# Two fold buffers, row-wise adds, whole K heads and planned idle in a two-layer decode kernel

## The chip, the core and the metric

The kernel runs on one core of a Trainium2 chip. Five engines work from instruction streams of their own and meet through semaphores: TensorE (PE in the profile; its weight loads are listed as PEld), VectorE (DVE), ScalarE (ACT), GpSimd (POOL) and SyncE (SP), which here only issues DMAs. The metric is the device time of one execution in microseconds (us).

## The reference

One decode step for four batch rows: attention over a long cache, a gated feed-forward block, and both once more with the same weights and the same cache. With the shapes filled in:

```python
# x (4,1,512); k_cache, v_cache (4, 8, 8192, 128); wq (512, 4096); wo (4096, 512)
# w_gate, w_up (512, 1792); w_down (1792, 512); all bf16
def _A_ref(x, k_cache, v_cache, wq, wo):          # 32 query heads, 8 K/V heads, Dh = 128
    q = (x @ wq).reshape(B, 1, 32, 128).transpose(0, 2, 1, 3)
    k = repeat(k_cache, 4, axis=1); v = repeat(v_cache, 4, axis=1)
    p = softmax(einsum("bhqd,bhkd->bhqk", q, k) * 128 ** -0.5)
    o = einsum("bhqk,bhkd->bhqd", p, v)
    return o.transpose(0, 2, 1, 3).reshape(B, 1, 4096) @ wo
def _B_ref(x, w_gate, w_up, w_down):
    return (silu(x @ w_gate) * (x @ w_up)) @ w_down
x = x + _A_ref(layernorm(x), ...)
x = x + _B_ref(layernorm(x), ...)
x = x + _A_ref(layernorm(x), ...)
x = x + _B_ref(layernorm(x), ...)
```

## The kernel before

**Tiling.** K and V of one batch row and one K/V head are 2 MiB. They are cut into two units of 1 MiB (`cp` 0 and 1, 8 KB in each of 128 partitions). A unit is written (layer, row, head, cp). A ring of 11 slots of 1 MiB (`pool`) holds units; four more slots lie in `wq_sb` and become free when the last query projection has read wq. `load_unit` fetches one unit, `load_both` fetches a whole head, two units with 16 KB in each partition, into two neighbouring slots: slot pairs are (0,1), (2,3) and so on, so the eleventh slot has no partner. Weights have places of their own (wo in four pieces, gate, up and down in two pieces each). A block is one layer and one row; the blocks run in the order `KSEQ`: (0,0), (0,1), (1,0), (0,2), (1,1), (0,3), (1,2), (1,3). Of each row's V the first three heads (six units, `KEPT`) stay in their slots from layer 0 until layer 1 has used them; they are loaded once.

**A block.** For each K unit, DVE transposes its two halves in place in 32x32 pieces (`k_pair`, L621), then PE multiplies them with the padded query `qpad` (32 matmuls, L633; called QK below). The scores of the whole block gather in four PSUM banks. `softmax` then takes maxima on DVE (L651), exponentials on ACT (L655), joins the maxima over partitions with a matmul against `same` (`g2`, L673), rescales (L691), transposes p on PE and copies it back on ACT (L700, L706), and forms the inverse sums (L715 to L731). Each V head is two units of eight matmuls (`v_group`, L787; called PV below), whose result is spread over four partition strips; `fold` on DVE adds the four strips into the buffer `red` under a mask (one L810 and three L813), `flip` on PE turns `red` into columns (L819), `nm` scales them (L828) and `oproj` multiplies with wo (L750). The very last head has no fold and multiplies the other way round (L773), and its second unit comes in two halves, so that the end is short. All four folds, flips and heads share the one buffer `red`.

**A chain.** When all eight heads of a layer 0 row are projected, `chain` runs serially on PE, DVE and ACT: `add_x` adds the residual (L931), then come a layer norm (L457 to L485), gate and up (L844), the gating (L862 to L883), down (L893), `add_x` again, another layer norm, the query projection for layer 1 (L493) and the padding of the query (L506, L533). Only then can QK of that row's layer 1 block run. `add_x` writes all four rows of XT each time, of which a chain uses its own. After block (1,3) the same feed-forward runs once for all rows and ends the kernel.

**What sets the order.** Two things. The string `ORDER` gives the order in which SyncE issues loads: each K and V stands for the next unit of `kseq` or `vload` (nothing more is issued for the second unit of a head fetched whole), q for wq, e for the last half unit, every other letter for the next weight piece. `VGROUPS` gives the order of V heads and marks with w those fetched whole. And `Plan` runs an event model of the kernel while it is being built: every step has an engine, an assumed duration, the steps it depends on and a priority; the earliest startable step of each engine is placed next, a free PSUM bank or slot is handed out on the way, and `emit` writes all instructions in the order of planned starts. So each engine's program order is fixed by the plan; `_Sync` adds the semaphore waits at emission. A load waits on SyncE until its slot's last reader is done, and all later loads queue behind it. Chain steps and softmax steps have the highest priority, but a step that has begun is never interrupted. In this order of emission nothing keeps a second fold from being written ahead of the first one's flip.

Of the kernel before, what the change touches and what calls it, by code (L numbers as in the profile page):

```python
# [4 lines left out]
ACTF = mybir.ActivationFunctionType  # L5
# [97 lines left out]
class Step:  # L103
    __slots__ = ("eng", "us", "deps", "fn", "prio", "take", "free", "start", "end", "loads", "slot_of", "slots", "pairs", "more")

    def __init__(self, eng, us, fn, deps, prio, take=None, free=None, pairs=0):
        self.eng, self.us, self.fn, self.prio = eng, us, fn, prio
        self.pairs = pairs
        self.deps = [d for d in deps if d is not None]
        self.take, self.free = take, free  # L110
        self.start = self.end = None
        self.slot_of = None
        self.slots = ()
        self.more = ()


class Plan:
# [6 lines left out]
    FETCH = 6.0  # L124

    def __init__(self, nslots, banks):
# [4 lines left out]
        self.bank = {}  # L131

    def add(self, eng, us, fn, deps, prio, take=None, free=None, pairs=0):
        s = Step(eng, us, fn, deps, prio, take, free, pairs)
        self.steps.append(s)
        return s
# [8 lines left out]
    def run(self):  # L145
# [12 lines left out]
        held = {}  # L158
        slots = {i: 0.0 for i in range(self.nslots)}
# [49 lines left out]

        def pump(now):  # L210
# [22 lines left out]
        left = len(self.steps)  # L233
        pump(0.0)
        while left:
            best = None
            for e in engines:
                cand = None
                for t, s in todo[e]:
                    if s.take is not None:  # L240
# [3 lines left out]
                        t = max(t, b)  # L244
                    at = max(t, free_at[e])
                    k = (at > free_at[e] + 1e-9, at if at > free_at[e] + 1e-9 else 0.0, s.prio[0])
# [5 lines left out]
            if li < len(self.loads):  # L252
                if not self.loads[li].slots:
                    nxt = sp_at
                else:
                    found = pick(self.loads[li])
                    nxt = found[0][0] if found is not None else None
            if best is None and nxt is None:
# [4 lines left out]
            at, s = best  # L263
            s.start = at
# [6 lines left out]
            if s.take is not None:  # L271
# [3 lines left out]
                self.bank[s.take] = b  # L275
            if s.free is not None:
# [11 lines left out]
    def emit(self):  # L288
        for s in sorted(self.steps + self.loads, key=lambda s: (s.start, s.prio[0])):
# [3 lines left out]
ORDER = ("qKKKKKVKKKKKKVKKKKdKVKVKKVKKKKVKKKVKVVVVKgKKVKKuVdVoVuogooVVKKKKKKKKKKVKKKKKKVVVVKVKKKVKVKKVKKKK"  # L293
         "VVVKKVVVVVVKVVVKVKKVVKKVKKKKKKKKKKKKKVVVVKKVVKVVVKKKKVVVVVVVVVVKVKKVVVKKKKKKKVVKKVKKKKVKKKKVKKKK"
         "KVVVVVVVVVVVVVVVVVKKVKKKKKKKKKKKKKKVVVVVVVVVVVVVVVVe")
KEPT = [6, 6, 6, 6]
NSLOT = 11
VGROUPS = ("006w 007w 004w 001w 003w 005w 002w 000w 016w 015w 014 013w 112w 011w 012w 017w 010w 121w 105w 107 101 104w 103 106 "
           "120 110w 023 027 021w 026w 025w 100w 130 024w 022w 020w 116 113 115 114 117 035 033 036 034w 032w 031 037w "
           "030 125w 123w 111w 131w 132 127w 124w 133w 134w 122 102 135w 137w 136 126")  # L300


def bass_interleave_layers__gqa_block_cached__swiglu_ffn__decode_kernel(
# [33 lines left out]
    with ExitStack() as es:  # L337
# [11 lines left out]
        tiny = sb("tiny", [P, 28], FP32)  # L349
# [3 lines left out]
        var = tiny[:, 9:13]  # L353
        rstd = tiny[:, 13:17]
        eps_sb = tiny[:, 17:18]
        gm = tiny[:, 18:19]
        gl = tiny[:, 19:20]
        cmask = tiny[:, 20:24]
        gm4 = tiny[:, 24:28]
        identf = sb("identf", [P, P], FP32)  # L360
        same = sb("same", [P, P], FP32)
# [5 lines left out]
        red = sb("red", [P, P], FP32)  # L367
        x0T = sb("x0T", [P, NQ, B], FP32)
        XT = sb("XT", [P, NQ, B], FP32)
        dT = sb("dT", [P, NQ, B], FP32)  # L370
# [9 lines left out]
        gs2 = sb("gs2", [P, FO * B], FP32)  # L380

# [35 lines left out]
        def setup_late():  # L417
            op("dve", lambda e: e.tensor_reduce(same[:, 0:32], identf[:].rearrange("p (c h) -> p h c", c=4),
                                                AX.X, ALU.add), reads=["identf"], writes=["same"])
            s0 = same[:]  # L420
            op("dve", lambda e: e.tensor_copy(s0[:, 32:P].rearrange("p (c h) -> p c h", h=32),
                                              bass.AP(tensor=s0.tensor, offset=s0.offset,
                                                      ap=[[s0.ap[0][0], P], [0, 3], [1, 32]])),
               reads=["same"], writes=["same"])
# [43 lines left out]
        def layer_norm(dep, tag):  # L468
# [6 lines left out]
            def square():  # L475
                op("dve", lambda e: e.tensor_tensor(dT[:], XT[:], over_nq(mean), ALU.subtract),
                   reads=["x", "mean"], writes=["dT"])
# [654 lines left out]
```

## Time and profile before

| | before |
|---|---|
| median of 3 runs | 643.45 us (642.36 to 643.55) |
| the profiled execution | 642.89 us |
| its span | 641.1 us |
| mean granted TensorE clock | 0.688 |
| from HBM through the DMA queue of SyncE | 257.18 MB |
| loads of K: 1 MiB each | 128 |
| loads of V: 2 MiB and 1 MiB | 34 and 35 (and two halves) |

The span runs from the first to the last instruction. Busy shares are means over the whole span. A group's row gives line, engine, operation, output from input, count, then total busy time in us and mean ns of one, then the idle time of the engine in front of it and what ended it. A row of a timeline gives start and length in us, engine, line and count, and in square brackets the idle time before it with what ended it. A row of SyncE's waits gives total us, times and longest.

### The profile page before, as it was taken

What the parts mean: (1) busy time and instruction counts of PE and PEld (TensorE: products, weight loads), DVE (VectorE), ACT (ScalarE), POOL (GpSimd) and SP (SyncE); (2) the same over time, 40 slices, a digit from 0 to 9 for tenths busy, and PEclk for the clock granted to TensorE, in tenths of its full rate; (3) what the DMA queues carried; (4) which work ended last, traced back from release to release, by engine and by line L of the source; (5) the groups of instructions that cost most, each with busy time, mean ns of one, the idle gap of its engine ahead of it and who ended that gap; (6) DMA issues with size and microseconds to landing.
All of it is one profiled execution on the core that took longest, in us unless ns stands there. A gap on an engine that the chain in (4) does not pass through costs nothing.

```text
span 641.1 us, 17218 instructions
## 1 busy us (share of the span) xinstructions
PE 451.4 (70%) x7882; PEld 207.6 (32%) x7882; DVE 451.7 (70%) x817; ACT 48.3 (8%) x114; POOL 1.6 (0%) x7
## 2 busy tenths in 40 slices
PE   2656666474777767679777766797757677976787
PEld 2211322133422322245322432362312335522345
DVE  2787885672599769646998857379988844798553
ACT  1000300030000300000300300000200200000300
POOL 0000000000000000000000000000000000000000
PEclk9866588565586678665767687576586875588575
DMA  8999999999999999999999999999999999999991
GB/s 362 422 421 410 420 423 423 403 401 392 383 398 410 421 422 426 423 423 406 410 420 420 422 425 429 417 406 421 419 408 421 406 420 415 331 413 427 427 416 53
DMA packets 36368, 258.27 MB, mean 403 GB/s; under 512 B 3396, under 2 KB 9288, under 8 KB 10568
## 3 DMA queue, kind: packets, MB, share of 16 engines
q1 hardware_dynamic: 36272, 257.18, 97.7%
q8 instruction: 61, 1.00, 0.6%
q14 instruction: 11, 0.09, 0.0%
q10 hardware_dynamic: 24, 0.01, 0.0%
HBM read 257.17 MB, written 0.00 MB: 401 GB/s over the span
## 4 chain that ended last, share of the span: by engine, by line
DMA 54%; DVE 22%; PE 16%; SPq 5%; issue 3%; DVEq 0%
DMA pool<-in_A_k_cache_dram 37%; DVE pool L621 15%; DMA pool<-in_A_v_cache_dram 14%; PE ps L633 5%; PE ps L787 5%; SPq L92 5%; DVE red L813 4%; DMA wd_sb<-in_B_w_down_dram 3%; DVE red L810 1%; PE ps L844 1%; PE ps L819 1%; PE ps L493 1%; PE ps L893 1%; PE ps L457 1%; PE ps L750 1%
## 5 line engine op out<-in xcount | busy, mean ns | idle before, releaser
L621 DVE STREAM_TRANSPOSE pool<-pool 128x1024 uint32<-128x1024 uint32 x244 | 288.1, 1221 | 49.4 <-DMA pool<-in_A_k_cache_dram 44.3
L633 PE MATMUL ps<-pool,qpad 32*32 32x512 bf16 x3904 | 217.6, 519 | 69.5 <-DVE pool L621 62.9
L633 PEld LDWEIGHTS ps<-pool,qpad 32*32 32x32 bf16 x3904 | 64.0, 106 | 203.0 <-DVE pool L621 136.3
L787 PE MATMUL ps<-pool,pp 128*32 128x512 bf16 x960 | 97.4, 526 | 32.9 <-DMA pool<-in_A_v_cache_dram 29.0
L813 DVE SCALAR_TENSOR_TENSOR red<-ps,tiny,red 128x128 f32<-128x128 f32 x189 | 66.3, 351 | 6.7
L810 DVE TENSOR_SCALAR red<-ps,tiny 128x128 f32<-128x128 f32 x63 | 21.4, 340 | 64.1 <-PE ps L787 53.7
L819 PE MATMUL ps<-sel,red 128*128 128x4 f32 x126 | 30.9, 318 | 46.5 <-DVE red L813 45.4
L819 PEld LDWEIGHTS ps<-sel,red 128*128 128x128 f32 x126 | 25.7, 256 | 78.4 <-DVE red L813 70.6
L655 ACT ACTIVATE pp<-ps,negm 128x512 bf16<-128x512 f32 x32 | 21.6, 685 | 304.2 <-DVE negm L651 297.4
L787 PEld LDWEIGHTS ps<-pool,pp 128*32 128x32 bf16 x960 | 22.3, 111 | 67.7 <-DMA pool<-in_A_v_cache_dram 39.9
L651 DVE TENSOR_REDUCE negm<-ps 128x1 f32<-128x512 f32 x32 | 19.8, 682 | 10.8 <-PE ps L633 10.8
L750 PE MATMUL ps<-oT,wo_sb 128*128 128x4 bf16 x640 | 21.9, 166 | 4.8 <-DVE oT L828 3.2
L750 PEld LDWEIGHTS ps<-oT,wo_sb 128*128 128x128 bf16 x640 | 21.2, 104 | 11.5 <-DVE oT L828 4.7
L493 PE MATMUL ps<-xnT,wq_sb 128*128 128x4 bf16 x640 | 18.4, 166 | 8.8 <-DMA wq_sb<-in_A_wq_dram 8.0
L493 PEld LDWEIGHTS ps<-xnT,wq_sb 128*128 128x128 bf16 x640 | 18.2, 104 | 10.9 <-DMA wq_sb<-in_A_wq_dram 8.1
L483 ACT ACTIVATE tiny<-tiny 128x4 f32<-128x4 f32 x10 | 3.0, 300 | 233.5 <-DVE tiny L463 233.5
L828 DVE TENSOR_TENSOR oT<-ps,invL 128x4 bf16<-128x4 f32 x64 | 9.7, 151 | 14.2 <-PE ps L819 13.3
L706 ACT ACTIVATE pp<-ps 128x1024 bf16<-128x1024 bf16 x16 | 16.1, 1023 | 29.4 <-PE ps L700 29.4
L700 PE MATMUL ps<-ident,pp 128*128 128x128 bf16 x128 | 14.9, 296 | 0.5 <-DVE invL L731 0.3
L700 PEld LDWEIGHTS ps<-ident,pp 128*128 128x128 bf16 x128 | 11.9, 137 | 9.1 <-DVE selw L719 4.2
L621 DVE STREAM_TRANSPOSE wq_sb<-wq_sb 128x1024 uint32<-128x1024 uint32 x12 | 14.2, 1224 | 0.5
L633 PE MATMUL ps<-wq_sb,qpad 32*32 32x512 bf16 x192 | 11.1, 516 | 4.9 <-DVE wq_sb L621 4.8
(73 smaller groups left out, 171.6 us busy)
## 6 DMA issues: line engine op xcount, KB each, us to landing
pool<-in_A_k_cache_dram SPq DMA_DIRECT2D x122, 1024.0 KB, 10.2
pool<-in_A_v_cache_dram SPq DMA_DIRECT2D x31, 2048.0 KB, 13.2
pool<-in_A_v_cache_dram SPq DMA_DIRECT2D x35, 1024.0 KB, 9.5
wq_sb<-in_A_k_cache_dram SPq DMA_DIRECT2D x6, 1024.0 KB, 12.6
wq_sb<-in_A_v_cache_dram SPq DMA_DIRECT2D x3, 2048.0 KB, 17.5
wq_sb<-in_A_wq_dram SPq DMA_DIRECT2D x1, 4096.0 KB, 12.5
wo_sb<-in_A_wo_dram SPq DMA_DIRECT2D x4, 1024.0 KB, 19.4
wg_sb<-in_B_w_gate_dram SPq DMA_DIRECT2D x2, 896.0 KB, 15.7
```

Of the source, the lines that this page charges most:

```text
L92: ins = self.eng[engname].dma_start(out_ap, in_ap)
L493: op("pe", lambda e: e.matmul(ps[:, bk * BW + h * B:bk * BW + (h + 1) * B], lhsT=wq_sb[:, kt, h * Dh:(h + 1) * Dh], rhs=xnT[:, kt * B:(kt ...
L621: op("dve", lambda e: e.transpose(v, v), reads=[key], writes=[key])
L633: op("pe", lambda e: e.matmul(ps[32 * c:32 * (c + 1), a * BW:(a + 1) * BW], lhsT=qpad[rows, es_, g, :], rhs=ap[h][rows, :, es_ // 2, :, es ...
L651: op("dve", lambda e: e.tensor_reduce(negm[:, q, a:a + 1], bank(a), AX.X, ALU.max, negate=True), reads=[f"pb{a}"], writes=[f"negm{q}_{a}"])
L655: op("act", lambda e: e.activation(pblk(q)[:, :, a, :], bank(a).rearrange("p (t j) -> p t j", j=32), ACTF.Exp, bias=negm[:, q, a:a + 1], s ...
L700: op("pe", lambda e: e.matmul(stg[:, t * P:(t + 1) * P], lhsT=pp[:, q, blk * P:(blk + 1) * P], rhs=ident[:], is_transpose=True, start=True ...
L750: op("pe", lambda e: e.matmul(ps[:, OPJ * BW + nq * B:OPJ * BW + (nq + 1) * B], lhsT=wo_sb[:, h, nq * P:(nq + 1) * P], rhs=o_cols(l, h), s ...
L787: op("pe", lambda e: e.matmul(ps[32 * j:32 * (j + 1), bk * BW:(bk + 1) * BW], lhsT=pp[:, q, at:at + 32], rhs=ap[:, 4 * j * Dh:4 * (j + 1) ...
L810: op("dve", lambda e: e.tensor_scalar(red[:], blk, mask4[:, t:t + 1], None, op0=ALU.mult), reads=[f"pb{bk}", "mask4"], writes=["red"])
L813: op("dve", lambda e: e.scalar_tensor_tensor(red[:], blk, mask4[:, t:t + 1], red[:], op0=ALU.mult, op1=ALU.add), reads=[f"pb{bk}", "mask4" ...
L819: op("pe", lambda e: e.matmul(ps[:, bk * BW:bk * BW + REP], lhsT=red[:], rhs=sel8[:, REP * (g % 2):REP * (g % 2 + 1)], start=True, stop=True),
```

## The change

- `red` gets a second half. A fold takes one of the two (`hold`) when it is planned and the flip gives it back (`drop`); a fold can be planned only when a half is free, and its half is free again when the flip ends.
- `add_x` gets the rows it may write: a chain's own row, and all four at the end. So in layer 0 each chain now leaves the other rows of XT as they are.
- To make room, `same` shrinks from 128 to 32 columns and one copy in the setup goes; `g2` becomes four matmuls of 32 columns, one for each partition strip. `var` and `dT` share places with `rstd` and `gs`.
- The K units of a block come head by head (cp 0 and 1 of one head together), and 25 K heads, all of layer 0, are loaded whole.
- The plan can leave an engine idle ahead of a step of a chain or a softmax: `LOOK` gives each of the four chains and eight softmaxes an index into `AHEAD`; a step that is in no such group isn't started when it would still be running at the expected start of a group's step that is less than so many us away. Four softmaxes have a value over 0: (0,0) 1.6, (1,0) 0.3, (1,1) 0.6, (1,3) 0.3; the chains have 0.
- `ORDER` and `VGROUPS` are new. Loads and bytes are the same in sum: 245.25 MiB through the queue. The stream now begins with wo0 and a whole K head ahead of wq. The last load of (0,3) ends at 209.25 MiB in both; after it came the V heads (1,2,5) and (1,2,3) and then the 16 K units of (1,3), and now come the heads (1,2,7), (1,2,5) and (1,2,3) with two of the K units among them, and then the other 14. The last K unit ended at 229.25 MiB and now ends at 231.25.

```diff
+        self.side = {}
+        self.ahead = [self.AHEAD[int(c)] for c in LOOK]      # AHEAD = (0.0, 0.3, 0.6, 1.0, 1.6)
...
+        def expected(s, depth):
+            t = 0.0
+            for d in s.deps:
+                x = d.end
+                if x is None:
+                    if depth == 0 or d.group is None:
+                        return None
+                    x = expected(d, depth - 1)
+                    if x is None:
+                        return None
+                    x = max(x, free_at[d.eng]) + d.us
+                t = max(t, x + (self.HOP if d.eng != s.eng else 0.0))
+            return t
+
+        def due():
+            found = {e: [] for e in engines}
+            for k, g in enumerate(self.groups):
...
+                    x = expected(s, 3)
+                    if x is not None:
+                        found[s.eng].append((x, self.ahead[k]))
+            return found
...
+                    if s.hold is not None:
+                        if not sides:
+                            continue
+                        t = max(t, min(sides.values()))
                     at = max(t, free_at[e])
+                    if s.group is None and any(at + s.us > x + 0.05 and x - at < w for x, w in soon[e]):
+                        continue
...
+            if s.drop is not None:
+                sides[self.side[s.drop]] = s.end + self.HOP
...
-ORDER = ("qKKKKKVKKKKKKVKKKKdKVKVKKVKKKKVKKKVKVVVVKgKKVKKuVdVoVuogooVVKKKKKKKKKKVKKKKKKVVVVKVKKKVKVKKVKKKK"
-         "VVVKKVVVVVVKVVVKVKKVVKKVKKKKKKKKKKKKKVVVVKKVVKVVVKKKKVVVVVVVVVVKVKKVVVKKKKKKKVVKKVKKKKVKKKKVKKKK"
-         "KVVVVVVVVVVVVVVVVVKKVKKKKKKKKKKKKKKVVVVVVVVVVVVVVVVe")
+ORDER = ("oKqKKKKKKKKKKKKKKVKKVKVVKVKVKKKKVKKVKVKVVKVVKVdoVKVuggouKodVKKKKKKKKKKKVKKVKKKVVVVVVKKVKKVKVKKVV"
+         "VVVKVVKVKKVVVKKKKKKVVKKVKKKKKKKKKKKKKKVVVVVVKVVKKKVKKVVKKKKKKKVVVVVVVVKKVVKKVVVVKKKKVKVKKKKKKKKKK"
+         "VVVVVVVVVVVVVVVVVVKVVVKKKKKKKKKKKKKKKVVVVVVVVVVVVVVe")
...
+LOOK = "000040102001"
+KWHOLE = "000 001 002 003 004 005 006 007 010 011 012 013 014 015 016 017 020 022 023 031 032 033 034 035 036"
...
-        red = sb("red", [P, P], FP32)
+        red = sb("red", [P, 2, P], FP32)
...
             def g2():
                 bk = pbk(n + "a")
-                op("pe", lambda e: e.matmul(ps[:, bk * BW:bk * BW + 4], lhsT=same[:], rhs=gm4[:], start=True, stop=True),
-                   reads=["gm4", "same"], writes=[f"pb{bk}"])
-            s = PL.add("pe", 0.51, g2, [s], CHAIN, take=n + "a", pairs=2)
+                for c in range(4):
+                    op("pe", lambda e: e.matmul(ps[32 * c:32 * (c + 1), bk * BW:bk * BW + 4], lhsT=same[:], rhs=gm4[:],
+                                                start=True, stop=True, tile_position=(0, 32 * c)),
+                       reads=["gm4", "same"], writes=[f"pb{bk}"], sig=(c == 3))
+            s = PL.add("pe", 0.6, g2, [s], CHAIN, take=n + "a", pairs=8)
...
             def fold():
-                bk = pbk(tag)
+                bk, r = pbk(tag), PL.side[tag]
...
-                        op("dve", lambda e: e.tensor_scalar(red[:], blk, mask4[:, t:t + 1], None, op0=ALU.mult),
-                           reads=[f"pb{bk}", "mask4"], writes=["red"])
+                        op("dve", lambda e: e.tensor_scalar(red[:, r, :], blk, mask4[:, t:t + 1], None, op0=ALU.mult),
+                           reads=[f"pb{bk}", "mask4"], writes=[f"red{r}"])
...
-                op("dve", lambda e: e.tensor_tensor(XT[:].rearrange("p n b -> p (n b)"), base[:].rearrange("p n b -> p (n b)"),
-                                                    ps[:, bk * BW:bk * BW + NQ * B], ALU.add),
+                got = ps[:, bk * BW:bk * BW + NQ * B].rearrange("p (n b) -> p n b", b=B)
+                op("dve", lambda e: e.tensor_tensor(XT[:, :, rows], base[:, :, rows], got[:, :, rows], ALU.add),
                    reads=[key, f"pb{bk}"], writes=["x"])
...
-        kseq = [("k", l, b, g, cp) for l, b in KSEQ for cp in range(NCP) for g in range(G)]
+        kseq = [("k", l, b, g, cp) for l, b in KSEQ for g in range(G) for cp in range(NCP)]
...
+        twin |= {("k",) + tuple(int(c) for c in x) for x in KWHOLE.split()}
```

## Predicted, before the changed kernel was run

> **What bounds the kernel now.** I read the page first (busy shares, the forty slices, the DMA queue, the chain that ended last), then the table of stages in 16 us and 4 us windows, SyncE's own timeline and waits, and last the timeline of two places: the end of layer 0's last batch row and the tail.
>
> ```profile
> span 641.1 us, 17218 instructions
> ...
> PE 451.4 (70%) x7882; PEld 207.6 (32%) x7882; DVE 451.7 (70%) x817; ACT 48.3 (8%) x114; POOL 1.6 (0%) x7
> ...
> GB/s 362 422 421 410 420 423 423 403 401 392 383 398 410 421 422 426 423 423 406 410 420 420 422 425 429 417 406 421 419 408 421 406 420 415 331 413 427 427 416 53
> ...
> q1 hardware_dynamic: 36272, 257.18, 97.7%
> ...
> DMA 54%; DVE 22%; PE 16%; SPq 5%; issue 3%; DVEq 0%
> ...
> L621 DVE STREAM_TRANSPOSE pool<-pool 128x1024 uint32<-128x1024 uint32 x244 | 288.1, 1221 | 49.4 <-DMA pool<-in_A_k_cache_dram 44.3
> ...
> pool<-in_A_k_cache_dram SPq DMA_DIRECT2D x122, 1024.0 KB, 10.2
> pool<-in_A_v_cache_dram SPq DMA_DIRECT2D x31, 2048.0 KB, 13.2
> ```
>
> No compute engine is over 70% and the DMA queue is busy 97.7%: this is one long stream from HBM. Its undisturbed rate is about 421 GB/s, so a MiB takes 2.49 us. At that rate 257.18 MB take 611 us; the rest of the span, 30 us, is the tail after the last byte (about 14: the last row below carries 80 GB/s x 16 us = 3.0 us of stream, so it ends near 627), the first slice (362, worth 2.2) and dips. The change moves no byte out of the stream, so it can only win in the dips, in the rate, or in the tail.
>
> ```profile
> 160.00:176.00 16.00, 11.92 (x279) 7.89 (x287) 7.92 (x20) 0.51 (x2) 0.00 (x0) 0.50 0.97 385
> 176.00:192.00 16.00, 11.99 (x240) 3.88 (x240) 15.88 (x14) 0.00 (x0) 0.00 (x0) 0.82 1.00 398
> ...
> 320.00:336.00 16.00, 11.10 (x201) 3.36 (x208) 15.28 (x15) 0.00 (x0) 0.00 (x0) 0.70 1.01 421
> ...
> 512.00:528.00 16.00, 12.20 (x138) 5.80 (x135) 8.43 (x30) 1.68 (x2) 0.00 (x0) 0.71 1.01 427
> ...
> 576.00:592.00 16.00, 9.72 (x208) 3.07 (x208) 15.11 (x13) 0.00 (x0) 0.00 (x0) 0.91 1.02 427
> 592.00:608.00 16.00, 11.32 (x107) 5.25 (x95) 7.96 (x25) 5.13 (x11) 0.00 (x0) 0.50 1.01 428
> 608.00:624.00 16.00, 13.57 (x194) 6.72 (x187) 9.37 (x30) 0.00 (x0) 0.00 (x0) 0.73 1.00 417
> 624.00:640.00 16.00, 11.91 (x315) 9.69 (x312) 5.90 (x25) 0.76 (x3) 0.00 (x0) 0.59 0.20 80
> ```
>
> The columns are PE, weight loads, DVE, ACT, POOL, granted clock, DMA share, GB/s. The deepest dip, the slice of 331, is layer 0's last chain, in 4 us windows:
>
> ```profile
> 544.00:548.00 4.00, 4.00 (x109) 2.76 (x106) 1.31 (x6) 0.05 (x1) 0.00 (x0) 0.50 0.75 252
> 548.00:552.00 4.00, 4.00 (x33) 1.63 (x27) 2.66 (x9) 0.00 (x0) 0.00 (x0) 0.50 0.96 332
> 552.00:556.00 4.00, 3.62 (x101) 3.42 (x99) 3.89 (x10) 0.51 (x2) 0.00 (x0) 0.50 1.01 371
> 556.00:560.00 4.00, 3.46 (x110) 2.09 (x115) 4.00 (x8) 0.00 (x0) 0.00 (x0) 0.50 0.98 389
> 560.00:564.00 4.00, 4.00 (x97) 1.55 (x81) 4.00 (x5) 0.00 (x0) 0.00 (x0) 0.76 0.98 365
> ```
>
> **Term 1, the dip of chain 3.** Against 421 these five windows miss 169, 89, 50, 32 and 56 GB/s; times 4 us over 421 that is 3.8 us. SyncE shows why:
>
> ```profile
> 533.05 1.45 SPq L92 DMA_DIRECT2D pool<-in_A_k_cache_dram  x1
> ...
> 546.09 5.79 SPq L92 DMA_DIRECT2D pool<-in_A_k_cache_dram  x4
> ```
>
> ```profile
> SPq L62 <- PE ps L787: 13.0, 2, 12.5
> ```
>
> Six of the 11 slots hold kept V units of row 3; after two 2 MiB V loads and one K the queue stands 12.5 us for a PV to free one, and nothing else is issued. The old order then has only K of (1,3), whose QK needs the chain's query; the new order places three V heads of (1,2) there (6 MiB instead of 4) among the first two K units. The first wait stays: five slots are five slots. But what two freed slots are given next is V that PE can use at once, so 2 MiB, up to 5.0 us of streaming, fall into the windows from 548 on, which miss 2.2 us. I take -2.0; ends 0 (PE is busy all 4.00 us of the first two windows and the PVs come no sooner) and -3.8.
>
> **Term 2, 25 whole K heads.** 25 loads of 2 MiB take the place of 50: 52.4 MB, of which each byte gets a better rate or not. With whole V heads in the stream I read 427 and 428, with single K 421: 52.4 MB differ by 1.9 us. But 576 to 592, where the last single K land, has 427 too. Ends 0 and -1.9; I take the middle, -1.0. The 25 issues saved on SyncE are hidden, since its queue runs ahead of the stream. A pair's first half is usable later: the 2 MiB rows land 13.2 us after issue against 10.2, so each first half sits some 2.5 to 3 us more in its slot. That is cover, not time, as long as pairs come free early (rival B).
>
> The Trainium skill, DMA: Bandwidth & Descriptors, "Why a DMA increments its semaphore by 16 and not by 1", says that only the full count of 16 means all data has landed, and an intermediate value doesn't tell which bytes have; so nothing of a pair can start before its last byte. The 13.2 against 10.2 agrees. It speaks against this part; by it alone term 2 would give nothing, the last K would land 1.0 later, and the sum would end at 642.2.
>
> **Term 3, other dips.** Chain 0, 160 to 192, misses 36 and 23 GB/s, 2.2 us. The weights and the end of wd1 stand at 61.25 MiB of the stream in both orders, and a V pair and single K of (1,0) follow in both. 0; ends -2.2 and +2.2. At the start wq now lands after 7 MiB, not 4 (+7.5 us), so the first QK moves from 19.6 to about 27:
>
> ```profile
> 19.60 3.40 PE L633 MATMUL ps<-pool,qpad 32*32 32x512 bf16 x64 [0.90 <-DVE qpad L533]
> ```
>
> By then 4.5 MiB of K have landed and 4 to 5 are in flight, inside 11 slots; DVE transposes meanwhile. 0; end +2.5 (one K unit late).
>
> **Term 4, the chain's own instructions.** The setup copy (L421) goes; row-wise adds keep their count, on a smaller tile; 0, and at most a tenth of a us over the kernel. The maximum over partitions (L673) turns from one 128-wide fp32 matmul, two passes, into four 32-wide ones, eight passes, in each of 8 softmaxes.
>
> ```profile
> L673 PE MATMUL ps<-tiny,same 128*128 128x4 f32 x16 | 4.5, 354 | 5.1 <-DVE tiny L667 5.1
> ...
> L506 PE MATMUL ps<-qT,ident 128*32 128x16 bf16 x256 | 3.5, 179 | 2.0 <-DVE qT L545 1.5 <-DVE qT L557 0.5
> ```
>
> The nearest 32-wide row costs 3.5 / 256 = 14 ns each in a burst, so six more cost +0.1; the other end is six at the old pace, 4.5 / 16 = 0.28 each, +1.7. I take +0.2, and only the last softmax's is on the path; the other seven lie under the stream.
>
> **Term 5, two fold buffers and planned idle.** In 'red' a second fold already runs ahead of the first flip:
>
> ```profile
> 532.16 1.12 DVE L813 SCALAR_TENSOR_TENSOR red<-ps,tiny,red 128x128 f32<-128x128 f32 x3
> ...
> 533.78 1.12 DVE L813 SCALAR_TENSOR_TENSOR red<-ps,tiny,red 128x128 f32<-128x128 f32 x3
> ...
> 534.96 0.59 PE L819 MATMUL ps<-sel,red 128*128 128x4 f32 x2 [1.53 <-DVE red L813]
> ```
>
> ```profile
> DVE red L810 <- PE ps L819: 9.8, 11, 3.1
> ```
>
> So the plan loses no freedom by the new rule; a flip no longer waits for a foreign fold, and 9.8 us of DVE waiting for flips go. Under the stream both are worth 0. So is the planned idle, at most 1.6 us ahead of a step, which holds the non-chain work behind it (transposes on DVE, QK and PV on PE). Without that cover it costs its own length. Where these count is the tail.
>
> **The tail decides how much of the gain is paid out.**
>
> ```profile
> 586.93 4.85 DVE L621 STREAM_TRANSPOSE wq_sb<-wq_sb 128x1024 uint32<-128x1024 uint32 x4
> 591.84 1.90 PE L633 MATMUL ps<-wq_sb,qpad 32*32 32x512 bf16 x31 [0.52 <-DVE wq_sb L621]
> 593.81 2.48 DVE L651 TENSOR_REDUCE negm<-ps 128x1 f32<-128x512 f32 x4 [2.02 <-PE ps L633]
> ...
> 606.27 3.60 PE L787 MATMUL ps<-pool,pp 128*32 128x512 bf16 x32
> ...
> 613.96 0.39 PE L819 MATMUL ps<-sel,red 128*128 128x4 f32 x2 [1.77 <-DVE red L813]
> ...
> 616.81 0.59 PE L819 MATMUL ps<-sel,red 128*128 128x4 f32 x2 [0.66 <-DVE red L813]
> ...
> 625.27 0.39 PE L819 MATMUL ps<-sel,red 128*128 128x4 f32 x2 [0.66 <-DVE red L813]
> ...
> 627.84 1.02 PE L773 MATMUL ps<-pp,pool 128*128 128x4 bf16 x32 [0.75 <-DMA pool<-in_A_v_cache_dram]
> ```
>
> From the last QK (end 593.7) run a softmax of 12.5 us to the first PV at 606.27, then eight V heads of (1,3) to the last V matmul at 627.84. That one waited for its DMA only 0.75 us: the engines alone would be ready at 627.1. So a faster stream is worth at most 0.75 us unless this block moves too. The stream: 627.84 - 3.0 (terms 1 and 2) = 624.8. The engines: from 592 on the rows carry 428, 417 and 80 GB/s x 16 us = 14.1 MiB, so the last K (16 MiB before the end of the stream) landed near 592 - 1.9 x 2.46 = 587.3, and its QK ended 6.4 later; two transposes (2.44) and one QK (1.90) would be 4.3. The new order puts the last K 2 MiB later: 587.3 + 5.0 - 3.0 = 589.3, plus 4.3 to 6.4, middle 5.35: 594.7, that is +0.9. Softmax: +0.2 (term 4), -0.6 for the planned idle of 0.3 and fewer PVs between its steps (ends 0 and -2.7: its listed steps and handovers come to some 9.8). Flips waiting for folds after 606 lose 1.77 + 0.66 + 0.66 = 3.1; two buffers save -2.0 (ends 0 and -3.1). 627.1 + 0.9 + 0.2 - 0.6 - 2.0 = 625.6, later than 624.8, so it sets the end: 627.84 - 625.6 = 2.2 us gained. What follows (projection, norm, FFN) is unchanged.
>
> **Sum.** The profiled execution took 642.89 (span 641.1 and 1.8 around it), 0.56 under the median of 643.45. 642.89 - 2.2 = 640.7; against the median **641.2**.
>
> **The rivals.** A, *the last K block comes too late*, slower. The stream gains nothing, the lag stays 6.4: the last QK ends 5.0 later, the softmax and flips save nothing, 627.1 + 4.9 = 632.0, +4.2: 647.6. For it: the 2 MiB move is certain. Against: two fold buffers and a lag that has 2 us of slack. It decides from a last QK past 594.5 (593.7 + 0.75). B, *pairs are late*: the eleventh slot has no partner and a pair is free only with its later half; a pair late once in 25 to 150 us idles the stream up to 4.9: 641.2 + 4.9 = 646.1. Against: the order leaves four pairs there, and a pair's own time (5.0 transfer, 4.9 transposes, 1.9 QK) needs 2.4. C, *hidden anyway*: the chain 3 dip stays because PE is full, whole K gain nothing: 643.2. D, *the plan mends more*: half of all dips go and the last block moves with them. 30 - 14 - 2.2 leaves 14; half is 7: 636.5. For it: dips of 383 to 410 stand in a dozen slices; against: some are weight loads that stay.
>
> **How the numbers follow.** Forecast 0.35, own range 638.5 to 643.5; A 0.20, B 0.12, C 0.20, D 0.13. The range takes in A and D with the unknown ends of terms 2 and 4: 634.5 to 649. A measurement of this kernel tells about 0.2% (1.3 us) from no change. Faster: 0.30 of the forecast, all of D, 0.05 of C: 0.48. Same: 0.05 of the forecast, 0.12 of C: 0.17. Slower: A, B, 0.03 of C: 0.35.
>
> **What would show it.** Term 1: the windows after the last (0,3) load over 380, with SyncE's wait on PV under 10 us. Term 2: slices 2 to 9 over 424. Tail: the wait of the last V matmul for its DMA near 0, last QK near 594, the last softmax under 12.3, few flips waiting on folds. Wrong: a slice under 390 before 110 us (B), a last QK past 596 (A), or the dip merely moved (C).

## The result and the profile after

The changed kernel took 638.05 us (median of 7 runs, 637.67 to 638.40); the kernel before, run beside it, 642.06 (7 runs). The ratio is 0.9937, with an interval of 0.9922 to 0.9953: 4.0 us faster, where the forecast of 641.2 against 643.45 was 2.25 faster. The profiled execution took 637.67, its span is 635.9 (before: 641.1) at the same mean clock of 0.688.

The page of the changed kernel, in the parts that were shown of before:

```profile
span 635.9 us, 17225 instructions
...
PE 452.9 (71%) x7930; PEld 205.6 (32%) x7930; DVE 449.6 (71%) x816; ACT 48.6 (8%) x114; POOL 1.6 (0%) x7
...
GB/s 349 430 426 427 425 426 427 404 399 393 383 416 407 421 426 426 421 409 421 418 409 420 423 427 424 428 423 383 416 419 419 425 423 422 414 403 425 425 421 48
...
q1 hardware_dynamic: 32816, 257.18, 97.7%
...
DMA 58%; PE 21%; DVE 17%; SPq 3%; issue 1%; ACT 0%; DVEq 0%
...
pool<-in_A_k_cache_dram SPq DMA_DIRECT2D x72, 1024.0 KB, 8.7
pool<-in_A_v_cache_dram SPq DMA_DIRECT2D x30, 2048.0 KB, 14.1
pool<-in_A_k_cache_dram SPq DMA_DIRECT2D x25, 2048.0 KB, 14.9
```

The same bytes and the same work on PE and DVE; the stream is still the bound. Slices 2 to 7 carry 425 to 430 where they carried 410 to 423, and the slice of 331 is gone. A new dip of 383 stands at 429 to 445 us. Chain 3 in the same five windows as in the prediction, then SyncE's timeline there:

```profile
544.00:548.00 4.00, 3.96 (x92) 2.21 (x90) 3.44 (x12) 0.25 (x1) 0.00 (x0) 0.50 1.02 403
548.00:552.00 4.00, 2.98 (x44) 1.73 (x40) 1.50 (x8) 0.00 (x0) 0.00 (x0) 0.50 0.99 410
552.00:556.00 4.00, 3.82 (x96) 3.19 (x89) 3.22 (x7) 0.51 (x2) 0.00 (x0) 0.50 1.01 422
556.00:560.00 4.00, 3.47 (x126) 2.24 (x132) 4.00 (x9) 0.00 (x0) 0.00 (x0) 0.50 0.94 352
560.00:564.00 4.00, 3.46 (x109) 1.54 (x91) 3.98 (x5) 0.00 (x0) 0.00 (x0) 0.61 1.00 418
```

```profile
534.10 0.33 SPq L92 DMA_DIRECT2D pool<-in_A_k_cache_dram  x1
535.54 5.87 SPq L92 DMA_DIRECT2D pool<-in_A_v_cache_dram  x3
546.04 7.00 SPq L92 DMA_DIRECT2D pool<-in_A_k_cache_dram  x4
```

Against 421 the windows miss 18, 11, 0, 69 and 3 GB/s, 1.0 us instead of 3.8. Before, nothing was issued from 534.5 to 546.1. Now a K unit goes out at 534.10 and three V units from 535.54 on, with waits of 1.1, 3.7 and 1.1 us between them (a row of the timeline merges its issues), and then the queue stands for 4.6 us, from 541.4 to 546.0. SyncE's waits from 520 to 546 us, whose row of before the prediction shows:

```profile
SPq L62 <- PE ps L853: 22.3, 4, 11.9
```

The longest, 11.9 us, is another one: it ends at 534.10, ahead of that K unit, while loads issued earlier are still landing. The tail, from the timeline:

```profile
591.22 1.08 PE L695 MATMUL ps<-wq_sb,qpad 32*32 32x512 bf16 x31 [0.61 <-DVE wq_sb L683]
592.37 2.48 DVE L714 TENSOR_REDUCE negm<-ps 128x1 f32<-128x512 f32 x4 [1.21 <-PE ps L695]
...
595.73 0.28 PE L737 MATMUL ps<-tiny,same 128*32 128x4 f32 x8
...
602.50 3.61 PE L853 MATMUL ps<-pool,pp 128*32 128x512 bf16 x32 [1.11 <-ACT pp L771]
...
609.65 0.39 PE L885 MATMUL ps<-sel,red 128*128 128x4 f32 x2 [0.36 <-DVE red L879]
...
616.76 0.39 PE L885 MATMUL ps<-sel,red 128*128 128x4 f32 x2 [0.32 <-DVE red L879]
...
621.51 0.95 PE L839 MATMUL ps<-pp,pool 128*128 128x4 bf16 x32 [0.18 <-DMA pool<-in_A_v_cache_dram]
623.44 0.55 PE L839 MATMUL ps<-pp,pool 128*128 128x4 bf16 x16 [0.97 <-DMA pool<-in_A_v_cache_dram]
...
624.69 0.59 PE L839 MATMUL ps<-pp,pool 128*128 128x4 bf16 x16 [0.47 <-DMA pool<-in_A_v_cache_dram]
```

The last QK ends at 592.3 (before 593.7), the softmax takes 10.1 us to the first PV (12.5), two flips wait for folds, 0.68 in sum (3.1), and PE then waits for the last three loads in turn: the stream sets the end. The last K unit landed at 588.8, before at 589.4; its two transposes start with the landing. The row of the changed kernel first, then that of before:

```profile
588.79 2.37 DVE L683 STREAM_TRANSPOSE wq_sb<-wq_sb 128x1024 uint32<-128x1024 uint32 x2
```

```profile
589.41 2.37 DVE L621 STREAM_TRANSPOSE wq_sb<-wq_sb 128x1024 uint32<-128x1024 uint32 x2
```

**Where along the stream the time was won.** Adding up GB/s in 4 us windows gives the time at which each kernel had fetched so many MiB. The lead over before at equal bytes, in us, for this kernel and the experiments below (profiled executions; the numbers of two executions of like kernels differ by up to about 1):

```
MiB fetched      55     115    195    225    245
after            1.60   1.37   1.46   5.30   5.29
k_single        -0.01  -9.07 -18.01 -14.4  -14.4
v_back           1.52          0.56   1.42   1.42
no_idle          1.48         -0.05   3.87   3.96
late_122         1.47          0.25   3.67   3.74
start_k          1.24         -0.46   3.65   3.65
mend_only       -0.20         -0.34   0.33   0.43
b_v_ahead       -0.24         -0.36  -2.85  -2.98
b_tail          -0.33         -0.08   0.75   0.70
mend_tail       -0.29         -1.32  -1.58  -1.68
mend_122_tail   -0.22         -0.68   0.20   0.15
one_red          1.64  -1.69 -12.0  -13.95
```

So 1.6 us come in the first 55 MiB and 3.8 between 195 and 225 MiB, which is layer 0's last chain. All of it is paid out: the lead of 5.3 is 5.2 of span. That holds for these two executions; the medians differ by 4.0, as the profiled execution of before took 0.8 more than the median of the runs beside the changed kernel and that of the changed kernel 0.4 less than its own.

### The profile page after: what moved, and what is told of

Its sections match the earlier page's. It is cut to its first block, busy times and chain, and to the rows that moved or that the text cites. A ratio compares the mean times of both kernels' runs of the same rounds, so it can differ in the third digit from the quotient of the medians.

```text
span 635.9 us, 17225 instructions
## 1 busy us (share of the span) xinstructions
PE 452.9 (71%) x7930; PEld 205.6 (32%) x7930; DVE 449.6 (71%) x816; ACT 48.6 (8%) x114; POOL 1.6 (0%) x7
## 4 chain that ended last, share of the span: by engine, by line
DMA 58%; PE 21%; DVE 17%; SPq 3%; issue 1%; ACT 0%; DVEq 0%
DMA pool<-in_A_k_cache_dram 38%; DMA pool<-in_A_v_cache_dram 17%; DVE pool L683 12%; PE ps L695 7%; PE ps L853 7%; DMA wq_sb<-in_A_v_cache_dram 3%; SPq L92 3%; DVE red L879 2%; PE ps L912 1%; DVE negm L714 1%; PE ps L885 1%; PE ps L765 1%; PE ps L519 1%; PE ps L816 1%; DVE red L876 1%
## 5 line engine op out<-in xcount | busy, mean ns | idle before, releaser
L695 PE MATMUL ps<-pool,qpad 32*32 32x512 bf16 x3904 | 222.7, 547 | 69.1 <-DVE pool L683 60.5
L853 PE MATMUL ps<-pool,pp 128*32 128x512 bf16 x960 | 99.8, 538 | 31.5 <-DMA pool<-in_A_v_cache_dram 27.9
L555 PE MATMUL ps<-xnT,wq_sb 128*128 128x4 bf16 x640 | 18.5, 166 | 16.6 <-DMA wq_sb<-in_A_wq_dram 16.0
L765 PEld LDWEIGHTS ps<-ident,pp 128*128 128x128 bf16 x128 | 12.5, 141 | 11.5 <-DVE pp L756 4.9
L525 DVE TENSOR_REDUCE tiny<-ps 128x4 f32<-128x16 f32 x20 | 3.4, 168 | 14.9 <-PE ps L519 14.9
## 6 DMA issues: line engine op xcount, KB each, us to landing
pool<-in_A_k_cache_dram SPq DMA_DIRECT2D x25, 2048.0 KB, 14.9
```

Of the source, the lines that this page charges most:

```text
L555: op("pe", lambda e: e.matmul(ps[:, bk * BW + h * B:bk * BW + (h + 1) * B], lhsT=wq_sb[:, kt, h * Dh:(h + 1) * Dh], rhs=xnT[:, kt * B:(kt ...
L695: op("pe", lambda e: e.matmul(ps[32 * c:32 * (c + 1), a * BW:(a + 1) * BW], lhsT=qpad[rows, es_, g, :], rhs=ap[h][rows, :, es_ // 2, :, es ...
L765: op("pe", lambda e: e.matmul(stg[:, t * P:(t + 1) * P], lhsT=pp[:, q, blk * P:(blk + 1) * P], rhs=ident[:], is_transpose=True, start=True ...
L853: op("pe", lambda e: e.matmul(ps[32 * j:32 * (j + 1), bk * BW:(bk + 1) * BW], lhsT=pp[:, q, at:at + 32], rhs=ap[:, 4 * j * Dh:4 * (j + 1) ...
```

## The experiments

Each ratio is to the kernel before in runs on the same chip (its medians there: 642.6 to 643.2), with its 95% interval.

### The edits alone, without the new order

`mend_only` is the changed kernel with the old `ORDER`, `VGROUPS` and order of K units, no whole K and no planned idle: the two fold buffers, row-wise adds and the new `g2` remain.

```diff
-LOOK = "000040102001"
-KWHOLE = "000 001 002 003 ... 036"
+LOOK = "000000000000"
+KWHOLE = ""
...
-        kseq = [("k", l, b, g, cp) for l, b in KSEQ for g in range(G) for cp in range(NCP)]
+        kseq = [("k", l, b, g, cp) for l, b in KSEQ for cp in range(NCP) for g in range(G)]
```

> The changed kernel with the load order, the K unit order, single K loads and an idle setting of 0 everywhere, as before: only the two fold buffers, the row-wise adds and the four 32-wide matmuls are left. Theory (they lie under the stream): 0 within 1.3 us, ratio 0.998 to 1.002, with the dip of 544 to 564 as before. Rival (two buffers free PE and DVE enough to matter): 2 us or more faster, ratio under 0.997, shorter from the last QK to the last V matmul.

Measured 642.55 us (12 runs), ratio 0.9996 [0.9981, 1.0012]: no difference. Its tail shows why, in the timeline of PE:

```profile
618.82 1.05 PE L853 MATMUL ps<-pool,pp 128*32 128x512 bf16 x16 [0.80 <-DMA pool<-in_A_v_cache_dram]
...
621.30 1.04 PE L853 MATMUL ps<-pool,pp 128*32 128x512 bf16 x8 [0.72 <-DMA pool<-in_A_v_cache_dram]
...
626.27 1.02 PE L839 MATMUL ps<-pp,pool 128*128 128x4 bf16 x32 [1.44 <-DMA pool<-in_A_v_cache_dram]
```

The last block now waits for its loads by 0.80, 0.72 and 1.44, where before only the last V waited, 0.75. The buffers take some 2 us out of PE's last block, and the stream, unchanged, eats them.

`one_red` leaves the changed kernel with the rule that a fold needs a free buffer, but one buffer:

```diff
-        sides = {0: 0.0, 1: 0.0}
+        sides = {0: 0.0}
```

> The changed kernel with one fold buffer kept by the plan in place of two: no fold is planned before the flip of the one before has ended. Theory (every fold now waits for a flip, PSUM banks and with them PVs and slots come free later): slower than the changed kernel by 3 to 12 us, ratio 0.998 to 1.012, with more idle time of DVE ahead of folds. Rival (fold and flip lie under the stream, as in mend_only): within 1.3 us of the changed kernel.

Measured 654.64 us (4 runs), ratio 1.0189 [1.0173, 1.0205], 16.6 us above the changed kernel. Its waits hold a line that the changed kernel's lack:

```profile
DVE red L876 <- PE ps L885: 12.4, 14, 2.1
```

Folds wait for foreign flips, SyncE's longest wait for a PV grows from 12.7 to 17.4 us, and slices fall to 338, 334 and 269 GB/s. The loss is larger than expected. The order was made for two buffers, so this is the price of the rule with one buffer in this order, not in an order made for one.

`no_idle` takes the planned idle out.

```diff
-LOOK = "000040102001"
+LOOK = "000000000000"
```

> The changed kernel with the idle setting 0 for all chains and softmaxes. Theory (planned idle is worth nothing under the stream and the last softmax keeps its length or gets up to 2 us longer, inside the slack of the last block): within 1.3 us of the changed kernel, ratio 0.992 to 0.9955, the last softmax (first maximum to first PV of (1,3)) 10 to 12.5 us. Rival (the idle ahead of the last softmax is what lets the tail follow the stream): 1.5 to 2.5 us slower, no DMA wait at the last V matmul, ratio 0.996 to 0.998.

Measured 638.16 us (6 runs), ratio 0.9929 [0.9911, 0.9948], as the changed kernel. Its last softmax takes 9.8 us, no longer than with the idle; in both no PV of a `pool` unit runs between the softmax steps, where before there were two.

### Whole K heads

`streams` measures the rate alone: loads and nothing else, in four stretches of 32 MiB: 1 MiB units with 4 in flight, whole heads with 2, units with 10, whole heads with 5.

```diff
+        single(heads[0:16], [0, 1, 2, 3])
+        whole(heads[16:32], [4, 6])
+        single(heads[32:48], list(range(10)))
+        whole(heads[48:64], [0, 2, 4, 6, 8])
```

> Loads alone, nothing computed and zeros written out: 32 MiB of single 1 MiB units with four in flight, 32 MiB of 2 MiB heads with two in flight, then the same with ten units and with five heads in flight. Theory (whole heads stream faster): 425 to 430 GB/s for whole heads in both depths against 418 to 423 for units. Rival (the rate depends on bytes in flight only): the same within 2 GB/s at equal depth, and the early gain has another cause.

The slices of its page (8.25 us each) and its landing times:

```profile
GB/s 291 427 425 420 423 421 421 423 421 395 308 431 431 429 429 427 431 425 433 324 362 429 424 421 421 422 420 426 416 327 348 429 431 427 431 427 429 429 427 290
...
pool<-in_A_k_cache_dram SPq DMA_DIRECT2D x32, 1024.0 KB, 9.9
pool<-in_A_k_cache_dram SPq DMA_DIRECT2D x16, 2048.0 KB, 9.8
pool<-in_A_v_cache_dram SPq DMA_DIRECT2D x32, 1024.0 KB, 24.8
pool<-in_A_v_cache_dram SPq DMA_DIRECT2D x16, 2048.0 KB, 24.5
```

The plateaus of the four stretches, in one execution: 422, 429, 422 and 429 GB/s. Between these two depths there is no difference, between the two sizes 1.6%. For the 52.4 MB of the 25 heads that is 52.4/0.422 - 52.4/0.429 = 2.0 us.

`k_single` is the changed kernel with every K in units.

```diff
-KWHOLE = "000 001 002 003 ... 036"
+KWHOLE = ""
```

> The changed kernel with its 25 whole K heads fetched as 50 single units, in the same order. Theory (52.4 MB at 422 instead of 429 GB/s as the loads alone showed): 2.0 us slower than the changed kernel, ratio to the kernel before about 0.997, the lead over the kernel before at 55 MiB down from 1.6 us to 0 to 0.5. Rival 1 (the early lead comes from the new order, which has no dip at 48 to 64 us): lead at 55 MiB stays over 1.0, ratio 0.993 to 0.995. Rival 2 (whole heads cost cover in the ring): faster than the changed kernel.

Measured 657.07 us (4 runs), ratio 1.0224 [1.0204, 1.0243]: 19 us above the changed kernel, far more than any rate explains. The stretch from 16 to 112 us shows the rate, the row of k_single first:

```profile
16.00:112.00 96.00, 61.66 (x1182) 24.42 (x1186) 71.82 (x92) 5.13 (x11) 0.00 (x0) 0.73 1.01 422
```

```profile
16.00:112.00 96.00, 64.74 (x1202) 24.63 (x1202) 71.58 (x92) 5.10 (x11) 0.00 (x0) 0.81 1.01 427
```

422 without and 427 with whole K, and the lead at 55 MiB falls from 1.6 to 0.0. The rest is lost in steps, the first of them here:

```profile
172.00:180.00 8.00, 6.86 (x138) 3.12 (x138) 6.55 (x13) 1.18 (x2) 0.00 (x0) 0.70 0.44 128
...
SPq L62 <- PE ps L695: 23.6, 5, 14.7
```

SyncE stands 14.7 us for a slot and the stream falls to 128 GB/s. The load that stands is a single unit, (1,0,1) cp 1 of K, and a QK frees its slot, at 175.8; in the changed kernel a PV frees the slot of the same load, at 168.2. So the edit changed which slot a unit takes. That this is what costs the rest is read off the two traces; the run does not isolate it.

### Chain 3

`v_back` is the changed kernel with the third V head put back behind the K units of (1,3); `b_v_ahead` is the kernel before with one more whole V head ahead of them.

```diff
-         "VVVVVVVVVVVVVVVVVVKVVVKKKKKKKKKKKKKKKVVVVVVVVVVVVVVe")
+         "VVVVVVVVVVVVVVVVVVKVKKKKKKKKKKKKKKKVVVVVVVVVVVVVVVVe")
```

```diff
-         "KVVVVVVVVVVVVVVVVVKKVKKKKKKKKKKKKKKVVVVVVVVVVVVVVVVe")
+         "KVVVVVVVVVVVVVVVVVVVVKKKKKKKKKKKKKKKKVVVVVVVVVVVVVVe")
```

> The changed kernel with one move: the second and last V head of (1,2) ahead of the K units of (1,3) goes back behind them, so 4 MiB of V stand there as in the kernel before, not 6, and the last K ends at 229.25 MiB again. Theory (what is issued into freed slots during chain 3 decides the dip): 2.0 to 3.5 us slower than the changed kernel, so 640 to 642 and a ratio to the kernel before of 0.997 to 1.000, with windows under 380 GB/s back between 544 and 564 us. Rival 1 (the dip shrank because folds and flips of the chain are no longer entangled, or since the chain came earlier): as the changed kernel, ratio 0.993 to 0.995. Rival 2 (the tail is bound by the engines, not by the stream): faster than the changed kernel, since its last K lands 2 MiB earlier.

> The kernel before with one move: the V head (1,2,7) goes ahead of the 16 K units of (1,3), so 6 MiB of V stand there, and the last K ends at 231.25 MiB. Theory: the dip of 544 to 564 us fills by 2 to 3.5 us and the stream ends that much earlier; the last V matmul waits for its DMA under 0.8 us or not at all, since the last K block moves later, and the time falls by 1 to 3 us, ratio 0.995 to 0.998. Rival 1 (the tail is bound by the engines with one fold buffer): the stream gains, the end does not, ratio 0.999 to 1.005 and no DMA wait at the last V matmul. Rival 2 (the dip is PE being full): neither moves, ratio 1.000.

v_back: 639.96 us (6 runs), ratio 0.9951 [0.9933, 0.9970]. That is 1.9 above the changed kernel by the medians, but 0.9 by the ratios, whose intervals overlap; the trace says more than the time. The dip is back, later:

```profile
552.00:556.00 4.00, 3.63 (x122) 3.64 (x123) 3.93 (x10) 0.00 (x0) 0.00 (x0) 0.50 0.68 281
556.00:560.00 4.00, 2.00 (x86) 1.47 (x92) 4.00 (x9) 0.51 (x2) 0.00 (x0) 0.50 0.66 176
```

The stream gains 0.9 from 195 to 225 MiB instead of 3.8, little more than the 0.7 of mend_only in the old order. So the V head ahead of the K units is needed. b_v_ahead: 647.44 us (6 runs), ratio 1.0071 [1.0048, 1.0094], slower than before, where a gain was expected. Its SyncE waits in this stretch, then its windows:

```profile
SPq L62 <- PE ps L787: 28.8, 5, 14.7
```

```profile
544.00:560.00 16.00, 13.88 (x296) 9.06 (x293) 6.96 (x27) 0.51 (x2) 0.00 (x0) 0.50 0.68 262
```

The whole head needs two neighbouring slots, waits 14.7 us for them, and the K units stand behind it in the queue. So a V head placed there is not enough. That the pair is what costs is only a reading: the next two runs have single units in that place and gain nothing either.

`b_tail` gives the kernel before the changed kernel's own order behind the last (0,3) load, with (1,2,7) whole and first; `mend_tail` does the same to mend_only. In this order one K unit stands among the three V heads, not two, and 15 follow.

```diff
-         "KVVVVVVVVVVVVVVVVVKKVKKKKKKKKKKKKKKVVVVVVVVVVVVVVVVe")
+         "KVVVVVVVVVVVVVVVVVKVVVKKKKKKKKKKKKKKKVVVVVVVVVVVVVVe")
...
-           "030 125w 123w 111w 131w 132 127w 124w 133w 134w 122 102 135w 137w 136 126")
+           "030 127w 125 123 111w 131w 132 124w 133w 134w 122 102 135w 137w 136 126")
```

> The kernel before with only the changed kernel's stretch after the last load of (0,3): V head (1,2,7) whole, then the heads (1,2,5) and (1,2,3) as single units with one K unit among them, then 15 K units, then (1,2,4). One fold buffer, no planned idle, single K loads, old order everywhere else. Theory (single units go into any slot that comes free while a pair blocks the queue until two neighbours are free, which is why moving a whole head there made it worse): the stream gains 2.5 to 3.5 us between 205 and 225 MiB. With one fold buffer the engines of the last block are late, so the end gains less than the stream: 0.5 to 2 us, ratio 0.997 to 0.9995, and the last V matmul waits for no DMA. Rival 1 (the gain needs the mended plan or whole K): the dip stays and the ratio is 1.000 or over. Rival 2 (the tail doesn't bind): the time falls by as much as the stream, ratio 0.9945 to 0.996.

> The run mend_only (two fold buffers, row-wise adds, four 32-wide matmuls; old order) with the same stretch. Theory: the stream gains 2.5 to 3.5 us as in b_tail, and since the two fold buffers left the last block about 3 us ahead of its loads in mend_only (waits for DMA of 0.80, 0.72 and 1.44 us), the end follows by 2 to 3 us: ratio 0.9955 to 0.997, better than b_tail. Rival (fold buffers don't matter): the same as b_tail within 0.1%.

b_tail: 645.89 us (12 runs, 642.97 to 649.07), 1.0049 [1.0030, 1.0068]; mend_tail: 643.62 (12 runs), 1.0013 [0.9997, 1.0029]. Neither gains, against both expectations. The profiled execution of b_tail is its fastest, so its trace shows the dip but not what the median lost. With the K units 2 MiB later and no faster stream, the last QK ends late, at 597.2 and 599.9: the mark of the prediction's rival A. SyncE and PE of b_tail, then PE of the changed kernel:

```profile
533.22 15.94 SPq L92 DMA_DIRECT2D pool<-in_A_v_cache_dram  x3
550.42 1.18 SPq L92 DMA_DIRECT2D pool<-in_A_k_cache_dram  x2
```

```profile
542.70 1.63 PE L844 MATMUL ps<-xnT,wu_sb 128*128 128x4 bf16 x56
544.26 1.04 PE L787 MATMUL ps<-pool,pp 128*32 128x512 bf16 x8
```

```profile
532.96 1.04 PE L853 MATMUL ps<-pool,pp 128*32 128x512 bf16 x8 [1.64 <-DMA pool<-in_A_v_cache_dram]
...
534.45 1.04 PE L853 MATMUL ps<-pool,pp 128*32 128x512 bf16 x8
...
538.49 1.04 PE L853 MATMUL ps<-pool,pp 128*32 128x512 bf16 x8
...
540.00 1.04 PE L853 MATMUL ps<-pool,pp 128*32 128x512 bf16 x8
540.98 0.59 PE L912 MATMUL ps<-xnT,wg_sb 128*128 128x4 bf16 x16
```

In b_tail the three V issues take 15.94 us instead of 5.87. The PVs of layer 1 that free slots run behind gate and up, from 544.26; in the changed kernel two of them, of (1,2,7), run ahead, at 538.49 and 540.00. Early PVs alone are not enough either; v_back has them too:

```profile
539.74 1.04 PE L853 MATMUL ps<-pool,pp 128*32 128x512 bf16 x8
...
541.25 1.04 PE L853 MATMUL ps<-pool,pp 128*32 128x512 bf16 x8
```

There the slots that they free go to K units, whose QK waits for the chain.

The loads, counted off against `ORDER` and `VGROUPS`, show one more difference. In the kernel before and in b_tail the last V head of row 3 to land is (0,3,0), a kept head, whose PVs free no slot. In the changed kernel it is (0,3,5), which is not kept: its two PVs, at 532.96 and 534.45, free the slots of the loads issued at 534.10 and 535.54, and the PVs of (1,2,7) free the next two. This is read off the traces; no run changes the order of these heads alone.

What makes the PVs of (1,2,7) early? `mend_122_tail` and `late_122` try the most visible difference, the place of kept head (1,2,2): the first plans it earlier in mend_tail, the second later in the changed kernel.

```diff
-           "120 110w 023 027 021w 026w 025w 100w 130 024w 022w 020w 116 113 115 114 117 035 033 036 034w 032w 031 037w "
+           "120 110w 023 027 021w 026w 025w 100w 130 024w 022w 020w 116 113 115 114 117 122 035 033 036 034w 032w 031 037w "
```

```diff
-           "037w 031w 032 030w 035w 127w 125 123 124w 134w 137w 135w 136w 102 133w 126")
+           "037w 031w 032 030w 035w 127w 125 123 124w 134w 137w 135w 136w 122 102 133w 126")
```

> The run mend_tail (two fold buffers, row-wise adds, four 32-wide matmuls, the new stretch of loads behind the last load of (0,3), old order elsewhere) with the kept head (1,2,2) moved to an early place in VGROUPS. Theory (it takes both: slots that come free before the chain, and V to put into them): the stream gains 2.5 to 4 us against mend_tail between 195 and 225 MiB, ratio 0.995 to 0.998 to the kernel before. Rival (whole K heads or planned idle are needed as well): ratio 1.000 or over, the dip stays.

> The changed kernel with one word moved in VGROUPS: the kept V head (1,2,2) goes back to the late place that it had before (behind (1,3,6)). It isn't loaded, so no load moves; only its PV gets a low priority, and in the plan the two slots that it holds come free 8 to 10 us later, in the chain of row 3. Theory (in the old order two slots stay with this head while the chain runs, so SyncE starves): the stream loses 2 to 3.5 us between 195 and 225 MiB, and the time is 1.5 to 3 us above the changed kernel, ratio 0.996 to 0.9985. Rival (the late PV is covered, the stretch of V and K loads alone decides): as the changed kernel, 0.993 to 0.995.

mend_122_tail: 642.46 us (12 runs), 1.0002 [0.9989, 1.0016]: one PV moves ahead of gate, to 539.96, the next runs at 544.44, and the stream gains 0.9 there, as in v_back. late_122: 638.12 (5 runs), 0.9928 [0.9917, 0.9940], gain kept. Both theories missed: the kept head is not the cause by itself.

### The start

`start_k` begins with the whole K head and wq, and loads wo0 only behind the first 18 MiB of the stream (its expectation says 15).

```diff
-ORDER = ("oKqKKKKKKKKKKKKKKVKKVKVVKVKVKKKKVKKVKVKVVKVVKVdoVKVuggouKodVKKKKKKKKKKKVKKVKKKVVVVVVKKVKKVKVKKVV"
+ORDER = ("KKqKKKKKKKKKKKKoKVKKVKVVKVKVKKKKVKKVKVKVVKVVKVdoVKVuggouKodVKKKKKKKKKKKVKKVKKKVVVVVVKKVKKVKVKKVV"
```

> The changed kernel with its first load moved: a whole K head first, then wq, and the first piece of wo, with rows of 1 KB, behind 15 MiB of the stream. PE's program is the same. Theory (the short rows cost at the start, where nothing else is in flight): the lead of the stream at 5 MiB rises from -0.5 to 0 us and the time falls by 0.3 to 0.7 us, at the edge of what can be told: ratio 0.992 to 0.9935. Rival (the start is hidden in the slack of the ring, or the short rows cost the same anywhere): no difference.

Measured 638.68 us (6 runs), ratio 0.9936 [0.9921, 0.9950]: the start is worth nothing that can be told either way. No version is clearly faster than the changed kernel.

## Why the prediction was right, and where it was short

The direction and the places were right: a stream-bound kernel that won in the dip of chain 3, in the rate of whole K and in a tail that passed the gain on. The sizes were not: 4.0 us were gained where 2.25 were forecast, and the tail passed all of it on for other reasons than those given. The time lies in the range, but 634.5 to 649 takes in nearly every case named, so that says little; it is 0.45 us below the likeliest case's own range of 638.5 to 643.5, and nearer to rival D's 636.5 than to 641.2.

- **Term 1** (-2.0, ends 0 and -3.8) was mis-sized: the five windows gain 2.8 and the stretch from 195 to 225 MiB 3.8 in the changed kernel, 3.4 to 4.1 in the three variants that keep the order of loads there. The step that failed is "the first wait stays: five slots are five slots", and with it "PE is busy ... and the PVs come no sooner".

  The row behind that step was also read wrongly: its 12.5 us ended at 531.8, ahead of the two V loads and the K, and the changed kernel has a like wait of 11.9. The wait that starved the stream came next, 11.5 us from 534.5 to 546.0. In the changed kernel it broke up into 1.1, 3.7, 1.1 and 4.6, because four slots came free from 534.0 to 541.1, behind PVs of (0,3,5) and (1,2,7), and three of them went to V; 544 to 548, held for lost, went from 252 to 403.

  Of the marks, a wait under 10 us holds for this wait, not for the row that was read, and windows over 380 for four of the five. The V moved ahead is necessary (v_back) but not sufficient (b_tail, mend_tail). The early PVs are not sufficient either, as v_back has them; that they are necessary is read from b_tail and mend_tail, which lack them, and no run moves them alone. What of the order ahead of 209 MiB brings them forward stays open: kept head (1,2,2) alone doesn't, and the order of the (0,3) heads wasn't tried apart from the rest.
- **Term 2** (-1.0, ends 0 and -1.9) was at its far end: 2.0 by the rates of streams, and 1.6 by the lead at 55 MiB, which covers only part of the heads. The window of 427 with single K, taken as doubt, was not the rate of single units: streams has them at 422 at both depths, and in the trace of before the single K units of that window land 2.48 us apart, which is 423. The Trainium skill's rule in DMA: Bandwidth & Descriptors, "Why a DMA increments its semaphore by 16 and not by 1", from which a time of 642.2 was worked out, cost nothing: whole K land after 14.9 us and units after 8.7, but slices 2 to 7 never starve.
- **Term 3** (0, ends ±2.2): with the 1.6 of the start taken off, the stream from 55 to 195 MiB gains -0.1 here and -1.0 to -1.7 in v_back, no_idle, late_122 and start_k. So small losses, among them the new dip at 429 to 445, inside the bounds; the start cost none.
- **Term 4** (+0.2) had the wrong sign. In the last softmax the eight passes took 0.28 us where the two took 0.59, both at a granted clock of 0.50.
- **Term 5**: 0 under the stream holds (mend_only, no_idle). Its clause "the plan loses no freedom by the new rule" holds for two buffers; with one, this order loses 16.6 us.
- **Tail.** "Engines set the end" failed. The last K was put at 587.3 from the bytes moved, and so the lag from the last K to its QK at 6.4 before and 5.35 after. By its landing it came at 589.4 before, with a lag of 4.4, the 4.3 that the sum had as its lower end.

  In the changed kernel it landed at 588.8, close to the forecast 589.3, and its QK ended at 592.3, 3.5 on, not at 594.7. Of the 1.4 us by which the last QK ends earlier than before, 0.6 are the landing and 0.8 luck: its 31 matmuls took 1.08 us at a granted clock of 0.90 to 0.95, before 1.90 at 0.50, and other executions of the new order have either.

  The softmax then lost 2.3 us, not 0.4, as no PVs of `pool` units stand between its steps: with two of them there it takes 10.5 to 12.5 us (before, mend_only, v_back), without them 9.4 to 10.1 (after, no_idle, late_122, start_k, b_tail, mend_tail, mend_122_tail). The planned idle has no part in that. The flips gave 2.4 (forecast 2.0). So the engines were ready at 621.3 instead of 625.6, and the stream, whose lead was 5.3 instead of 3.0, paid out in full.

Of the rivals, A's mark (a last QK past 596) and B's (a slice under 390 before 110 us, the first slice of the start aside) did not appear here, and C's dip did not stay. D said that the plan mends more: the last block did move, but half of all dips did not go.

## What to carry to other kernels

Where a load queue stands for slots, find the reader that frees the next one and ask what it runs behind on its engine. Here PVs ahead of a chain's matmuls and V loads to put into the slots that they free gained 3.8 us of stream together; either without the other gained 0.9 at most. Size a rate by the plateau of a whole load size, not by one window. And compute the end for engines and stream separately, each with its own term: slack won on the one that isn't last buys nothing until the other gains too (mend_only). Take the arrival of a load from its landing, not from the bytes moved: here the two lay 2.1 us apart.

## What the runs showed of the hardware

In streams the rate went by the load's shape and not by the depth: loads of 1 MiB, 8 KB in each of 128 partitions, ran at 422 GB/s and loads of 2 MiB, 16 KB in each, at 429, with 4 MiB and with 10 MiB in flight. Size and bytes per partition change together here. The Trainium skill, DMA: Bandwidth & Descriptors, "Measured", gives 341 GB/s for 1 MB and 425 for 16 MB, for loads issued by GpSimd. With several loads in flight from SyncE the fall at 1 MB does not appear.

Four fp32 matmuls of 32 columns in four column tiles (eight passes) took 0.28 us in the last softmax of the changed kernel, two passes of 128 columns 0.59 before; in the trace the first four of the eight start within 9 ns. The Trainium skill, TensorE: Matmul & The Clock Gate, "The mechanism" in its part on row and column tiling, says that matmuls in different tiles overlap, with starts some 4 ns apart; the trace agrees.
